# Results of attention on 64x32 places of the array, and the attention's two PSUM banks as separate tiles until the weights are decoded

## The chip, the core and the metric

The kernel runs on one core of one Trainium2 chip. A core has five engines with their own instruction queues: PE (TensorE, matmuls and transposes; its weight loads are listed as PEld), DVE (VectorE), ACT (ScalarE), POOL (GpSimd) and SP (SyncE), which here issues every DMA. They wait for each other through semaphores, and each works through its own instructions in the order in which they were written. Matmuls write to PSUM, eight banks of 128 partitions by 512 fp32 columns; DVE and ACT read and write PSUM too. The metric is the time of one execution on the device, in microseconds (us).

## The reference

Attention of 8 batches with 8 heads, 576 positions and head dimension 64, under a mask: in the first four heads a position sees itself and the 31 before it, in the last four every fourth of the 128 positions up to itself. The result, one row of 512 numbers per position, goes through a layer of two matmuls with a rational function between them:

```python
scores = scale * np.matmul(q, k.transpose(0, 1, 3, 2))
scores = np.where(masks[None], scores, -1e9)
attn = np.exp(scores - np.max(scores, axis=-1, keepdims=True))
attn = attn / (np.sum(attn, axis=-1, keepdims=True) + 1e-09)
x = np.matmul(attn, v)          # then (4608, 512)
h = x @ w_in                    # (4608, 2048)
P = a[0] + a[1] * h + a[2] * h**2 + a[3] * h**3
Q = 1.0 + np.abs(b[0]) * np.abs(h) + np.abs(b[1]) * h**2
out = (P / (Q + 1e-06)) @ w_out # (4608, 512)
```

w_in and w_out come as doubles, which the kernel turns into pairs of fp32 numbers itself (a decode of bit operations).

## The kernel before, in words

**Attention.** Each batch has six units (each 192 positions of 4 heads). A unit goes through a fixed chain: its q, k and v are loaded; PE multiplies q by k (scores); DVE adds the mask, takes the maximum and subtracts it (in some units of batches 0 and 1, PE adds the mask, and ACT takes the exponentials straight from PSUM); ACT takes exponentials, DVE sums and inverts (`recip`, lines 367 and 368); POOL normalizes (`norm`); PE transposes the weights (`transposes`, line 377); ACT or DVE copies them to SBUF (`place`, the tile p_T); PE multiplies v by them (`av`, the result); ACT and DVE split the result into a high part xh and a rest xl. Results of one unit and scores of the next are one step on PE. In batches 0 and 1 (`ROWS = 2`) a place holds two heads and the matmuls use all 128 rows and 64 columns of the array. From batch 2 on ("rows" units) two half arrays of 64 rows work side by side, each writing a bank of its own: the scores on places of 64 rows by 32 columns (eight at once), the results on places of 64 by 64 (four at once). These matmuls are fp32; the trace lists each as two weight loads and two matmuls.

**Two banks.** The scores and the transposes use the bank "att", the results the bank "dec". Batch 0 uses other banks too, for overlap. "dec" is also where DVE decodes the weights: a weight of 128x512 takes a scale on ACT, then `w_shift` (line 607), `w_low` and `w_sign` on DVE (in the trace the last two have the helper's line 216: `pair<-wi_raw,pair` and `wi_f<-wi_raw,pair`). att and dec are the two halves of one PSUM tile named `pair`; the framework sets semaphore waits by tile. The rows units need both halves as one tile, since DVE and ACT treat them with one instruction.

**The layer.** 144 tiles, each one of nine chunks of 512 positions by one of sixteen blocks of 128 hidden units: 12 matmuls for h, a chain on ACT, DVE and POOL for the rational function, 12 matmuls into four output banks (out0 to out3).

**The order.** All steps are put to a planner (`Plan`), which simulates the engines with costs that stand in the code and writes each engine's instructions in the order it finds. Its tables (`DUE`, `LATE`, `SLACK`) give ranks, `PLACE` tells which engine copies p_T, `EARLY_TILES` in how many tiles POOL may take a copy. SP's DMAs stand in one queue too. Helpers record most operations, so matmuls have line 207, ACT's line 210, DVE's lines 213 and 216, POOL's line 219, DMAs line 204.

Of the kernel before, what the change touches and what calls it, by code (L numbers as in the profile page):

```python
# [8 lines left out]
F32 = mybir.dt.float32  # L9
# [9 lines left out]
P = 128  # L19
# [6 lines left out]
BOTH, ON_ACT, ON_DVE = {"ACT": 450, "DVE": 500}, {"ACT": 450}, {"DVE": 500}  # L26


ON_PE = [[1, 0, 0, 1, 1, 1], [1, 0, 1, 1, 1, 0], [0, 0, 0, 0, 0, 0], [0, 0, 0, 0, 0, 0], [0, 0, 0, 0, 0, 0], [0, 0, 0, 0, 0, 0], [0, 0, 0, 0, 0, 0], [0, 0, 0, 0, 0, 0]]
PLACE = [(ON_ACT, ON_DVE), (ON_ACT, ON_ACT), (ON_ACT, ON_ACT), (ON_ACT, ON_DVE), (ON_ACT, ON_DVE), (ON_ACT, ON_DVE), (ON_ACT, ON_DVE), (ON_ACT, ON_DVE)]  # L30
DUE = [(1.15, 0.77), (7.09, 0.53), (31.18, 3.35), (45.13, 2.24), (56.94, 2.08), (78.73, 2.4), (94.03, 1.97), (106.25, 0.46)]

LATE = {"ab": -18.93, "ql": -5.42, "pl": 8.78, "qq": 10.97, "t1": 2.93, "t2": -2.65, "ln": -22.56, "ex": -6.33, "g0": 2.2, "g1": 0.06, "g2": -8.94, "gh": -36.44, "gl": 12.6, "out": 3.9}
SLACK = {"sc": -0.4, "qk0": 0.75, "v0": 0.39, "load": -2.47, "wi": 1.95, "wo": 0.71, "w": 0.5, "gl": 0.63, "out": 2.59}

EARLY_TILES = 40

ROWS = 2
LEFT = S - 512
# [38 lines left out]
class Plan:  # L78
# [3 lines left out]
    HOP = {"PE": 200.0, "ACT": 135.0, "DVE": 120.0, "POOL": 80.0, "SP": 0.0}  # L82
    TO_POOL, DUE_HOP, WINDOW = 70.0, 150.0, 100.0
    DMA_START, DMA_NS, DMA_RATE = 4000.0, 1600.0, 405.0
    PERIOD = 4082.0

    def __init__(self):
        self.ops, self.tags = [], {}
# [87 lines left out]
def tile_attention_moe(  # L176
# [17 lines left out]
    att = ctx.enter_context(tc.tile_pool(name="att", bufs=1))  # L194
    psum = ctx.enter_context(tc.tile_pool(name="psum", bufs=1, space=bass.MemoryType.PSUM))

    pin = tc.keep_in_program_order
    plan = Plan()  # L200
    op = plan.op
# [4 lines left out]
    def mm(o, lhs, rhs, start=True, stop=True):  # L206
        pin(nc.tensor.matmul(o, lhs, rhs, start=start, stop=stop))  # L207
# [44 lines left out]
    class Unit:  # L252
# [24 lines left out]

        def bank(self, tag, what):
            if tag in PAIR:
                return pair[:, PAIR[tag]]  # L280
            return psum.tile([P, 512], F32, tag=tag, name=f"{what}{self.n}", bufs=PS_BUFS[tag])

        def scores(self, tag, masked):
# [11 lines left out]
                mm(ps[64 * h : 64 * h + 64, cols], q_t[:, h, j, :], k_t[:, h, 32 * j : 32 * j + 64], start=not masked, stop=not masked or j == 5)  # L295

        def scores_rows(self):
            q_t = self.q.rearrange("p (g i c) -> p g i c", g=4, i=3)
            k_t = self.k.rearrange("p (g k) -> p g k", g=4)
            for i in range(3):  # L300
                for g in range(4):
                    for r in range(2):
                        half = slice(64 * r, 64 * r + 64)
                        mm(pair[32 * g : 32 * g + 32, r, 64 * i : 64 * i + 64], q_t[half, g, i], k_t[half, g, 32 * i : 32 * i + 64])

        def masks(self):
            for j, cnt, at in MASK_AT[self.u]:
# [11 lines left out]

        def blocks(self):  # L320
            if self.rows:
                return pair[:, :, :192].rearrange("p r (i k) -> p r i k", k=64)
            return self.s[:, :384].rearrange("p (j k) -> p j k", k=64)

        def small(self, tag):
# [62 lines left out]
        def av(self, tag):  # L388
            v_t = self.v.rearrange("p (i h e d) -> p i h e d", i=3, h=2, e=2)
            if self.rows:  # L390
                for i in range(3):
                    for h in range(2):
                        for e in range(2):
                            for r in range(2):
                                half = slice(64 * r, 64 * r + 64)
                                c0, c1 = 192 + 96 * h + 32 * i, 64 * h + 32 * e
                                mm(pair[64 * e : 64 * e + 64, r, c0 : c0 + 32], v_t[half, i, h, e, :], pT_rows[half, i, c1 : c1 + 32])
                return
            self.o = ps = self.bank(tag, "o_ps")
# [40 lines left out]
        def src(self, cols):  # L440
            first, cnt = cols
            if self.rows:
                o = pair[:, :, 192:384].rearrange("p r (h t) -> p h r t", h=2)
                if cnt > 96:
                    assert cnt == 192
                    return o
                r, t = divmod(first, 96)
                return o[:, :, r, t : t + cnt]
            return self.o[:, :384].rearrange("p (h t) -> p h t", h=2)[:, :, first : first + cnt]
# [14 lines left out]
        def plan(self, by, start):  # L464

            b, u = self.b, self.u
# [4 lines left out]
            rows = self.rows  # L471
            cold = 1.06 if start else 1.0
# [11 lines left out]
            ready = [lq, lk] + ([masked, identity] if on_pe else [])  # L484
            assert not (rows and on_pe)
            cost = 250 * on_pe
            scores = self.scores_rows if rows else lambda: self.scores(s_tag, on_pe)

            prev, Unit.open = Unit.open, None
            clear = []  # L490
            if prev and prev.rows != rows:
                clear = [close(prev), *decoded]
                prev = None
            if prev:
                sc = op({"PE": 1250 if rows else 1750 + cost}, 0, lambda e: (prev.av(prev.o_tag), scores()), *prev.placed, prev.lv, *ready)
                clear = prev.finish(sc)
            else:
                sc = op({"PE": 800 if rows else 1050 * cold + cost}, 0, lambda e: scores(), *ready, *clear)
            if on_pe:
                ma = mx = op({"DVE": 545}, 0, lambda e: self.max_bank(), sc)  # L500
                su = ex = sm = op({"ACT": 1750}, 0, lambda e: self.exp_bank(pp, pt), mx)
# [68 lines left out]

    def close(u):

        av = op({"PE": 800 if u.rows else 1050}, 0, lambda e: u.av(u.o_tag), *u.placed, u.lv)
        av.slack = 0.0
        eh, el = u.finish(av)
        if u.rows:
            plan.takes(av, "att", 1, [el])
        return el
# [24 lines left out]

    def w_shift(key):

        wb[key] = b = pair[:, PAIR["dec"]]
        pin(nc.vector.tensor_scalar(b.bitcast(I32), wf[key].bitcast(I32), 3, None, ALU.logical_shift_left))  # L607

    def w_low(key):
# [52 lines left out]
    class Tile:  # L662
# [8 lines left out]
        def h(self):  # L671
            xh, xl = x_tiles(self.c)
            w = wt["wi", self.ft]
            if self.bank in PAIR:
                ps = pair[:, PAIR[self.bank]]
            else:
                ps = psum.tile([P, 512], F32, tag=self.bank, name=f"h{self.i}", bufs=PS_BUFS[self.bank])
            self.ps = ps
            for kt in range(NK):
                wh, wl = w[:, 0, kt * P : (kt + 1) * P], w[:, 1, kt * P : (kt + 1) * P]  # L680
                mm(ps, wh, xh[:, kt, :], start=(kt == 0), stop=False)
                mm(ps, wh, xl[:, kt, :], start=False, stop=False)
                mm(ps, wl, xh[:, kt, :], start=False, stop=(kt == NK - 1))
# [113 lines left out]


    PAIR = {"att": 0, "dec": 1}
    pair = psum.tile([P, 2, 512], F32, name="pair")  # L800
    mask_t = const.tile([P, len(STRIP), 64], BF16, name="mask_t")
    ident = const.tile([P, P], F32, name="ident")
    ident_b = const.tile([P, P], BF16, name="ident_b")
# [166 lines left out]
```

## Time and profile before

| | |
|---|---|
| time, median of 3 runs | 968.23 us (966.24 to 968.71) |
| profiled execution, its own time | 968.85 us |
| its span (first to last instruction) | 967.0 us |
| PE busy | 917.1 us, 95% |
| PEld busy | 743.2 us, 77% |
| DVE busy | 707.3 us, 73% |
| ACT busy | 692.4 us, 72% |
| POOL busy | 464.8 us, 48% |
| mean granted PE clock | 0.975 |
| results of rows units, matmuls | 1728 records, 32.5 us |
| scores of rows units, matmuls | 1728 records, 26.1 us |

Busy time is a union: overlapping instructions of one engine count once. In rows of waits, "A <- B: total, times, longest" means that A's engine stood idle before A until B was done. In rows of the timeline the idle time before an instruction stands in brackets with what ended it. Times of POOL are rough, and the ends of matmuls are modelled; their starts are recorded.

### The profile page before, as it was taken

What the parts mean: (1) busy time and instruction counts of PE and PEld (TensorE: products, weight loads), DVE (VectorE), ACT (ScalarE), POOL (GpSimd) and SP (SyncE); (2) the same over time, 40 slices, a digit from 0 to 9 for tenths busy, and PEclk for the clock granted to TensorE, in tenths of its full rate; (3) what the DMA queues carried; (4) which work ended last, traced back from release to release, by engine and by line L of the source; (5) the groups of instructions that cost most, each with busy time, mean ns of one, the idle gap of its engine ahead of it and who ended that gap; (6) DMA issues with size and microseconds to landing.
All of it is one profiled execution on the core that took longest, in us unless ns stands there. A gap on an engine that the chain in (4) does not pass through costs nothing.

```text
span 967.0 us, 19505 instructions
## 1 busy us (share of the span) xinstructions
PE 917.1 (95%) x7645; PEld 743.2 (77%) x7645; DVE 707.3 (73%) x1273; ACT 692.4 (72%) x1205; POOL 464.8 (48%) x404
## 2 busy tenths in 40 slices
PE   6578789899999999999999999999999999999998
PEld 5465667678888877888888888888888888888876
DVE  5767789967877778778577776777677676657565
ACT  4666668866767677777777778767777777777765
POOL 3445456755555444444544445444454454444542
PEclk9977889999999999999999999999999999999999
DMA  9642560002332222311022121222112000001001
GB/s 335 252 150 68 192 269 22 1 20 72 116 116 82 70 73 72 110 48 66 1 81 71 38 73 44 73 72 72 43 74 72 18 22 23 1 1 45 0 1 44
DMA packets 26012, 72.53 MB, mean 75 GB/s; under 512 B 3008, under 2 KB 3904, under 8 KB 25920
## 3 DMA queue, kind: packets, MB, share of 16 engines
q1 hardware_dynamic: 25920, 71.28, 21.2%
q8 instruction: 60, 0.98, 0.4%
q14 instruction: 32, 0.26, 0.1%
HBM read 60.79 MB, written 10.49 MB: 74 GB/s over the span
## 4 chain that ended last, share of the span: by engine, by line
PE 75%; DVE 7%; ACT 3%; DMA 2%; POOL 1%; issue 1%; SPq 0%; POOLq 0%; ACTq 0%; DVEq 0%
PE out L207 34%; PE h L207 34%; PE pair L207 6%; DMA wo_raw<-in_w_out_dram 2%; DVE a L216 2%; PE pair L377 1%; ACT r L210 1%; DVE h L216 1%; DVE pair L216 1%; POOL a L219 1%; DVE pair L607 1%; DVE t L213 1%; DVE wo_f L216 1%; DVE xl L213 0%; ACT xh L210 0%
## 5 line engine op out<-in xcount | busy, mean ns | idle before, releaser
L207 PE MATMUL h<-xh,wi 128*128 128x512 f32 x1136 | 382.0, 398 | 12.7 <-DVE a L216 12.6
L207 PE MATMUL out<-gh,wo 128*128 128x512 f32 x1136 | 360.7, 399 | 1.0 <-POOL wo L219 0.8
L219 POOL TENSOR_TENSOR a<-r,a 128x512 f32<-128x512 f32 x141 | 182.1, 1291 | 321.8 <-ACT r L210 283.8
L207 PEld LDWEIGHTS h<-xh,wi 128*128 128x128 f32 x1136 | 216.0, 190 | 65.9 <-DVE a L216 18.9
L207 PEld LDWEIGHTS out<-gh,wo 128*128 128x128 f32 x1136 | 210.9, 190 | 44.9 <-POOL wo L219 1.1
L207 PE MATMUL h<-xl,wi 128*128 128x512 f32 x568 | 224.1, 395 | 0.0
L207 PE MATMUL out<-gl,wo 128*128 128x512 f32 x568 | 223.3, 393 | 0.0
L219 POOL TENSOR_TENSOR gl<-a,gh 128x512 fp32r<-128x512 f32 x141 | 184.3, 1307 | 25.3 <-ACT gh L210 22.7
L216 DVE SCALAR_TENSOR_TENSOR a<-a,r 128x512 f32<-128x512 f32 x141 | 98.9, 702 | 116.6 <-ACT r L210 115.4
L210 ACT ACTIVATE a<-h 128x512 f32<-128x512 f32 x140 | 83.5, 597 | 105.7 <-PE h L207 96.7
L216 DVE SCALAR_TENSOR_TENSOR h<-h,na_t,r 128x512 f32<-128x512 f32 x142 | 107.0, 754 | 50.2 <-ACT r L210 50.1
L210 ACT ACTIVATE r<-a,ln_bias 128x512 f32<-128x512 f32 x141 | 102.0, 723 | 56.3 <-POOL a L219 55.8
L207 PEld LDWEIGHTS out<-gl,wo 128*128 128x128 f32 x568 | 107.8, 190 | 23.2
L207 PEld LDWEIGHTS h<-xl,wi 128*128 128x128 f32 x568 | 108.1, 190 | 21.8 <-DVE xl L213 0.4
L210 ACT ACTIVATE r<-a,ab_t 128x512 f32<-128x512 f32 x141 | 114.6, 813 | 5.3 <-DVE a L216 3.2
L213 DVE TENSOR_TENSOR t<-t,h 128x512 f32<-128x512 f32 x142 | 96.8, 681 | 20.9 <-ACT t L210 19.5
L210 ACT ACTIVATE t<-h,na_t 128x512 f32<-128x512 f32 x142 | 109.6, 772 | 1.5 <-PE h L207 1.5
L216 DVE SCALAR_TENSOR_TENSOR h<-t,na_t,h 128x512 f32<-128x512 f32 x142 | 107.0, 754 | 3.9
L210 ACT ACTIVATE r<-r,exp_bias 128x512 f32<-128x512 f32 x144 | 103.9, 722 | 3.9
L210 ACT ACTIVATE gh<-a 128x512 fp32r<-128x512 f32 x126 | 79.5, 631 | 31.7 <-PE out L207 25.9
L216 DVE SCALAR_TENSOR_TENSOR a<-a,h 128x512 f32<-128x512 f32 x140 | 95.6, 683 | 2.8
L219 POOL TENSOR_TENSOR p<-p,sm 128x384 f32<-128x384 f32 x48 | 40.2, 837 | 60.8 <-DVE sm L368 34.3
(103 smaller groups left out, 720.3 us busy)
## 6 DMA issues: line engine op xcount, KB each, us to landing
v<-in_vp_dram SPq DMA_DIRECT2D x48, 384.0 KB, 3.4
qk<-in_qk_rows_dram SPq DMA_DIRECT2D x36, 448.0 KB, 4.7
out_dram<-os SPq DMA_DIRECT2D x36, 256.0 KB, 2.2
wi_raw<-in_w_in_dram SPq DMA_DIRECT2D x16, 512.0 KB, 8.6
wo_raw<-in_w_out_dram SPq DMA_DIRECT2D x16, 512.0 KB, 9.1
qk<-in_qk_dram SPq DMA_DIRECT2D x6, 608.0 KB, 4.7
q<-in_qk_dram SPq DMA_DIRECT2D x6, 384.0 KB, 6.9
k<-in_qk_dram SPq DMA_DIRECT2D x6, 224.0 KB, 7.0
```

Of the source, the lines that this page charges most:

```text
L207: pin(nc.tensor.matmul(o, lhs, rhs, start=start, stop=stop))
L210: pin(nc.scalar.activation(o, i, func, **kw))
L213: pin(nc.vector.tensor_tensor(o, x, y, op))
L216: pin(nc.vector.scalar_tensor_tensor(o, x, s, y, op0, op1))
L219: pin(nc.gpsimd.tensor_tensor(o, x, y, op))
L377: pin(nc.tensor.transpose(self.t[:, P * i : P * i + P], pf[:, P * i : P * i + P], ident))
L607: pin(nc.vector.tensor_scalar(b.bitcast(I32), wf[key].bitcast(I32), 3, None, ALU.logical_shift_left))
```

## The change

Four things change.

1. `av` of the rows units uses 64x32 places: the 64 rows of a result's half are two matmuls of 32 columns each, on two places, so 48 matmuls in the code in place of 24. They write the same numbers to the same places of PSUM, in an order that goes over the eight places.
2. att and dec are two tiles of a pool of their own as long as units of batches 0 and 1 and the decode use them (`two_banks` without `joined`). At the first scores of a rows unit that pool is closed and one tile of two banks is opened in its place (`join_banks`).
3. In batches 3 to 7 the copy of p_T goes from ACT to DVE (`PLACE`; the rows units use only the first entry).
4. The planner's tables and some of its costs have other numbers, and `EARLY_TILES` is 48.

```diff
-PLACE = [(ON_ACT, ON_DVE), (ON_ACT, ON_ACT), (ON_ACT, ON_ACT), (ON_ACT, ON_DVE), (ON_ACT, ON_DVE), (ON_ACT, ON_DVE), (ON_ACT, ON_DVE), (ON_ACT, ON_DVE)]
+PLACE = [(ON_ACT, ON_DVE), (ON_ACT, ON_ACT), (ON_ACT, ON_DVE), (ON_DVE, ON_ACT), (ON_DVE, ON_ACT), (ON_DVE, ON_ACT), (ON_DVE, ON_ACT), (ON_DVE, ON_ACT)]
...
-EARLY_TILES = 40
+EARLY_TILES = 48
...
-    PERIOD = 4082.0
+    PERIOD = 4051.0
...
+    early_banks = ExitStack()
+    apart = early_banks.enter_context(tc.tile_pool(name="psum_apart", bufs=1, space=bass.MemoryType.PSUM))
...
         def bank(self, tag, what):
             if tag in PAIR:
-                return pair[:, PAIR[tag]]
+                return two_banks(tag, f"{what}{self.n}", self.rows)
...
         def scores_rows(self):
+            join_banks()
...
-                        for e in range(2):
+
+                        for n in range(4):
                             for r in range(2):
-                                half = slice(64 * r, 64 * r + 64)
+                                half, e, d = slice(64 * r, 64 * r + 64), n // 2, slice(32 * (n % 2), 32 * (n % 2) + 32)
                                 c0, c1 = 192 + 96 * h + 32 * i, 64 * h + 32 * e
-                                mm(pair[64 * e : 64 * e + 64, r, c0 : c0 + 32], v_t[half, i, h, e, :], pT_rows[half, i, c1 : c1 + 32])
+                                mm(pair[0][32 * n : 32 * n + 32, r, c0 : c0 + 32], v_t[half, i, h, e, d], pT_rows[half, i, c1 : c1 + 32])
...
-        wb[key] = b = pair[:, PAIR["dec"]]
+        wb[key] = b = two_banks("dec", "%s_b%d" % key, False)
...
-    pair = psum.tile([P, 2, 512], F32, name="pair")
+    pair = []
+
+    def two_banks(tag, name, joined):
+        if not joined:
+            return apart.tile([P, 512], F32, tag=tag, name=name, bufs=1)
+        join_banks()
+        return pair[0][:, PAIR[tag]]
+
+    def join_banks():
+        if not pair:
+            early_banks.close()
+            late = ctx.enter_context(tc.tile_pool(name="psum_joined", bufs=1, space=bass.MemoryType.PSUM))
+            pair.append(late.tile([P, 2, 512], F32, name="pair"))
```

How the order and the waits move is shown at three places. In brackets stand the semaphores for which an instruction waits: DVE, PE, Activation, Pool, and DMAHW for loads.

**PE, the fourth unit of batch 1:** transposes (line 377, after the change 381), the first output group of a tile, results. Before:

```order
L377 MATMUL pair<-ident,p_911 128x128 [waits DVE_49,Pool_49]
L377 MATMUL pair<-ident,p_911 128x128 x2
L207 MATMUL out_0_0_676<-gh_894,wo_951 128x512 [waits Activation_49]
L207 MATMUL out_0_0_676<-gh_894,wo_951 128x512 [waits Pool_49]
L207 MATMUL out_0_0_676<-gl_927,wo_951 128x512
L207 MATMUL pair<-p_T,v_892 64x64 [waits DMAHW2_49,DVE_49]
```

With the change:

```order
L381 MATMUL t_ps_981<-ident,p_939 128x128 [waits Pool_49]
L381 MATMUL t_ps_981<-ident,p_939 128x128 x2
L210 MATMUL out_0_0_703<-gh_919,wo_978 128x512 [waits Activation_49]
L210 MATMUL out_0_0_703<-gh_919,wo_978 128x512 [waits Pool_49]
L210 MATMUL out_0_0_703<-gl_952,wo_978 128x512
L210 MATMUL o_ps_998<-p_T,v_917 64x64 [waits DMAHW2_49,DVE_49,Activation_49]
```

The order is the same. The transposes no longer wait for DVE, only for POOL's normalization; the results wait for ACT's copies by name, which before stood behind DVE's wait.

**DVE, the same time:** the last steps of one weight's decode and the three steps of the next (the weights' numbers differ between the kernels). Before:

```order
L216 SCALAR_TENSOR_TENSOR pair<-wo_raw_542,pair 128x512 [waits DMAHW1_49]
L216 SCALAR_TENSOR_TENSOR wo_f_802<-wo_raw_542,pair 128x512 [waits DVE_49]
L216 SCALAR_TENSOR_TENSOR h_819<-h_819,na_t,r_886 128x512 [waits Activation_49]
L607 TENSOR_SCALAR pair<-wi_f_834 128x512 [waits DVE_49]
L216 SCALAR_TENSOR_TENSOR pair<-wi_raw_544,pair 128x512 [waits DMAHW2_49,DVE_49,PE_49]
L216 SCALAR_TENSOR_TENSOR wi_f_834<-wi_raw_544,pair 128x512 [waits DVE_49,Activation_49]
```

With the change:

```order
L219 SCALAR_TENSOR_TENSOR wo_f_657<-wo_raw_549,wo_b_954 128x512
L612 TENSOR_SCALAR wi_b_976<-wi_f_837 128x512 [waits DVE_49]
L219 SCALAR_TENSOR_TENSOR h_848<-h_848,na_t,r_911 128x512 [waits Activation_49]
L219 SCALAR_TENSOR_TENSOR wi_b_976<-wi_raw_560,wi_b_976 128x512 [waits DMAHW2_49,DVE_49]
L219 SCALAR_TENSOR_TENSOR wi_f_837<-wi_raw_560,wi_b_976 128x512 [waits DVE_49]
```

The second step lost its wait for PE (the transposes), the third its wait for ACT (the copies of p_T). In the same way ACT's first copy of p_T waits for DVE before and for PE with the change.

**PE, the second rows unit:** results (p_T and v) and scores (qk) between output groups. Before:

```order
L207 MATMUL out_0_0_1405<-gl_2104,wo_1743 128x512 [waits Pool_49]
L207 MATMUL pair<-p_T,v_1268 64x32 [waits DMAHW1_49]
L207 MATMUL pair<-p_T,v_1268 64x32 x23
L207 MATMUL pair<-qk_1854 32x64 [waits DMAHW6_49]
L207 MATMUL pair<-qk_1854 32x64 x23
L207 MATMUL out_1_0_1414<-gh_2084,wo_1743 128x512 x2
```

With the change:

```order
L210 MATMUL out_0_0_1449<-gl_2164,wo_1795 128x512 [waits Pool_49]
L210 MATMUL pair<-p_T,v_1307 32x32 [waits DMAHW1_49]
L210 MATMUL pair<-p_T,v_1307 32x32 x47
L210 MATMUL pair<-qk_1914 32x64 [waits DMAHW6_49]
L210 MATMUL pair<-qk_1914 32x64 x23
L210 MATMUL out_1_0_1458<-gh_2144,wo_1795 128x512 x2
```

The result's 24 matmuls are 48, each with 32 columns of weights and 32 columns streamed; the place in the order is the same.

More of the change, by code (lines that the diff above doesn't have):

```diff
@@ L29 @@
 ON_PE = [[1, 0, 0, 1, 1, 1], [1, 0, 1, 1, 1, 0], [0, 0, 0, 0, 0, 0], [0, 0, 0, 0, 0, 0], [0, 0, 0, 0, 0, 0], [0, 0, 0, 0, 0, 0], [0, 0, 0, 0, 0, 0], [0, 0, 0, 0, 0, 0]]
-PLACE = [(ON_ACT, ON_DVE), (ON_ACT, ON_ACT), (ON_ACT, ON_ACT), (ON_ACT, ON_DVE), (ON_ACT, ON_DVE), (ON_ACT, ON_DVE), (ON_ACT, ON_DVE), (ON_ACT, ON_DVE)]
-DUE = [(1.15, 0.77), (7.09, 0.53), (31.18, 3.35), (45.13, 2.24), (56.94, 2.08), (78.73, 2.4), (94.03, 1.97), (106.25, 0.46)]
-LATE = {"ab": -18.93, "ql": -5.42, "pl": 8.78, "qq": 10.97, "t1": 2.93, "t2": -2.65, "ln": -22.56, "ex": -6.33, "g0": 2.2, "g1": 0.06, "g2": -8.94, "gh": -36.44, "gl": 12.6, "out": 3.9}
-SLACK = {"sc": -0.4, "qk0": 0.75, "v0": 0.39, "load": -2.47, "wi": 1.95, "wo": 0.71, "w": 0.5, "gl": 0.63, "out": 2.59}
-EARLY_TILES = 40
+PLACE = [(ON_ACT, ON_DVE), (ON_ACT, ON_ACT), (ON_ACT, ON_DVE), (ON_DVE, ON_ACT), (ON_DVE, ON_ACT), (ON_DVE, ON_ACT), (ON_DVE, ON_ACT), (ON_DVE, ON_ACT)]
+DUE = [(1.14, 0.78), (7.17, 0.52), (31.12, 3.35), (44.26, 2.11), (55.98, 1.84), (78.88, 1.84), (93.23, 1.71), (104.69, 0.27)]
+LATE = {"ab": -19.97, "ql": -10.42, "pl": 5.4, "qq": 18.68, "t1": 4.2, "t2": -2.51, "ln": -22.56, "ex": -3.7, "g0": 1.26, "g1": 0.06, "g2": -6.38, "gh": -35.31, "gl": 12.35, "out": 3.53}
+SLACK = {"sc": -0.4, "qk0": 0.66, "v0": 0.33, "load": -2.47, "wi": 2.03, "wo": 0.71, "w": 0.79, "gl": 0.63, "out": 2.59}
+EARLY_TILES = 48
 ROWS = 2
@@ L303, in scores_rows @@
                         half = slice(64 * r, 64 * r + 64)
-                        mm(pair[32 * g : 32 * g + 32, r, 64 * i : 64 * i + 64], q_t[half, g, i], k_t[half, g, 32 * i : 32 * i + 64])
+                        mm(pair[0][32 * g : 32 * g + 32, r, 64 * i : 64 * i + 64], q_t[half, g, i], k_t[half, g, 32 * i : 32 * i + 64])
         def masks(self):
@@ L321, in blocks @@
             if self.rows:
-                return pair[:, :, :192].rearrange("p r (i k) -> p r i k", k=64)
+                return pair[0][:, :, :192].rearrange("p r (i k) -> p r i k", k=64)
             return self.s[:, :384].rearrange("p (j k) -> p j k", k=64)
@@ L442, in src @@
             if self.rows:
-                o = pair[:, :, 192:384].rearrange("p r (h t) -> p h r t", h=2)
+                o = pair[0][:, :, 192:384].rearrange("p r (h t) -> p h r t", h=2)
                 if cnt > 96:
@@ L494, in plan @@
             if prev:
-                sc = op({"PE": 1250 if rows else 1750 + cost}, 0, lambda e: (prev.av(prev.o_tag), scores()), *prev.placed, prev.lv, *ready)
+                sc = op({"PE": 1370 if rows else 1750 + cost}, 0, lambda e: (prev.av(prev.o_tag), scores()), *prev.placed, prev.lv, *ready)
                 clear = prev.finish(sc)
             else:
-                sc = op({"PE": 800 if rows else 1050 * cold + cost}, 0, lambda e: scores(), *ready, *clear)
+                sc = op({"PE": 720 if rows else 1050 * cold + cost}, 0, lambda e: scores(), *ready, *clear)
             if on_pe:
@@ L571, in close @@
     def close(u):
-        av = op({"PE": 800 if u.rows else 1050}, 0, lambda e: u.av(u.o_tag), *u.placed, u.lv)
+        av = op({"PE": 1020 if u.rows else 1050}, 0, lambda e: u.av(u.o_tag), *u.placed, u.lv)
         av.slack = 0.0
@@ L674, in h @@
             if self.bank in PAIR:
-                ps = pair[:, PAIR[self.bank]]
+                ps = two_banks(self.bank, f"h{self.i}", True)
             else:
```

## The prediction

> **What bounds the kernel now.** I read the page's slices first, then the busy time by stage, then the waits of the first 222 us, then the timeline where those waits sit. The two rows of the page (40 slices of 24.2 us):
>
> ```profile
> PE   6578789899999999999999999999999999999998
> PEclk9977889999999999999999999999999999999999
> ```
>
> PE is full from the tenth slice on; before it, it idles, and its granted clock falls. By stage (busy us and instructions of each engine, then clock, DMA share, GB/s):
>
> ```profile
> 0.00:109.00 109.00, 76.37 (x717) 60.30 (x719) 72.64 (x152) 67.00 (x189) 49.34 (x58) 0.83 0.53 187
> 109.00:131.00 22.00, 18.76 (x109) 14.99 (x106) 18.10 (x36) 13.93 (x25) 12.80 (x12) 0.82 0.95 358
> 131.00:200.00 69.00, 59.71 (x291) 45.68 (x289) 63.61 (x103) 55.71 (x91) 44.83 (x36) 0.98 0.13 49
> 200.00:962.00 762.00, 761.15 (x6533) 621.62 (x6534) 552.91 (x985) 554.18 (x900) 357.82 (x299) 1.00 0.16 52
> ```
>
> Four stages. Up to 109 us nothing is full: PE 70%, DVE 67%, ACT 61%. A chain of single steps through the attention units sets the pace. From 109 to 131 us the last weights come in (DMA 95%). From 131 to 200 us DVE decodes them (63.6 of 69 us). From 200 us PE has no gap (761.2 of 762). So a microsecond won ahead of 109 us moves all that follows, and after 200 us only PE's own work counts.
>
> What the units wait for in the first 222 us (total us, times, longest us):
>
> ```profile
> PE pair L377 <- DVE pair L607: 7.0, 4, 2.8
> PE pair L377 <- DVE pair L216: 4.3, 1, 4.3
> DVE pair L216 <- PE pair L377: 4.6, 3, 2.8
> ACT p_T L210 <- DVE pair L216: 4.7, 4, 1.9
> DVE pair L607 <- ACT p L210: 4.0, 2, 2.0
> PE pair L207 <- DVE wi_f L216: 3.0, 2, 1.8
> PE pair L207 <- DVE wo_f L216: 1.2, 2, 0.8
> ```
>
> L377 transposes into the att bank; L607 and "DVE pair L216" write the dec bank. Neither needs the other's data: they wait because both banks are one tile. The last two rows, the results in dec waiting for a weight's last decoding step, are true ones and stay.
>
> **The early stage.** The fourth unit of batch 1 shows how such waits chain (start, us, engine, line):
>
> ```profile
> 87.55 0.83 POOL L219 TENSOR_TENSOR p<-p,sm 128x384 f32<-128x384 f32 x1 [2.08 <-DVE sm L368]
> 89.30 0.69 DVE L607 TENSOR_SCALAR pair<-wi_f 128x512 int32<-128x512 int32 x1
> 90.13 0.88 PE L377 MATMUL pair<-ident,p 128*128 128x128 f32 x3 [2.81 <-DVE pair L607]
> 91.04 0.69 DVE L216 SCALAR_TENSOR_TENSOR pair<-wi_raw,pair 128x512 int32<-128x512 int32 x1 [1.06 <-PE pair L377]
> 91.77 0.98 ACT L210 ACTIVATE p_T<-pair 64x384 f32<-64x384 f32 x2 [1.90 <-DVE pair L216]
> 92.78 0.69 DVE L216 SCALAR_TENSOR_TENSOR wi_f<-wi_raw,pair 128x512 int32<-128x512 int32 x1 [1.05 <-ACT p_T L210]
> 93.53 1.55 PE L207 MATMUL pair<-p_T,v 128*64 128x64 f32 x24 [1.24 <-DVE wi_f L216]
> ```
>
> The normalized weights are there at 88.38, the transposes start at 90.13. Then decode step, copies, decode step go one behind the other, though the copies and the decode have nothing in common. With two tiles the transposes start at about 88.45, the three decode steps run back to back from 89.30 (3 x 0.69, to 91.4), the copies run beside them, and the results start at 91.4 in place of 93.53: 2.1 us. The same in the first, third and fifth unit:
>
> ```profile
> 42.92 0.83 POOL L219 TENSOR_TENSOR p<-p,sm 128x384 f32<-128x384 f32 x1 [1.75 <-ACT r L210]
> 45.38 0.87 PE L377 MATMUL pair<-ident,p 128*128 128x128 f32 x3 [4.32 <-DVE pair L216]
> 48.05 1.55 PE L207 MATMUL pair<-p_T,v 128*64 128x64 f32 x24 [1.79 <-DVE wi_f L216]
> ...
> 68.34 0.70 DVE L607 TENSOR_SCALAR pair<-wi_f 128x512 int32<-128x512 int32 x1 [1.95 <-ACT p L210]
> 70.39 0.19 DVE L368 RECIPROCAL sm<-sm 128x6 f32<-128x6 f32 x1
> 72.02 0.52 PE L377 MATMUL pair<-ident,p 128*128 128x128 f32 x3 [2.36 <-DVE pair L607]
> ...
> 102.96 0.83 POOL L219 TENSOR_TENSOR p<-p,sm 128x384 f32<-128x384 f32 x1 [5.01 <-DVE sm L368]
> 104.25 0.52 PE L377 MATMUL pair<-ident,p 128*128 128x128 f32 x3 [0.99 <-DVE pair L607]
> 107.29 1.55 PE L207 MATMUL pair<-p_T,v 128*64 128x64 f32 x24 [0.77 <-DVE wo_f L216]
> ```
>
> First unit: inputs at 43.75, transposes at 45.38, so 1.6 us. Third: the shift sat 1.95 us behind exponentials that read the other bank, and the reciprocal, the normalization and the transposes queue behind it; they come about 2 us earlier, and PE's own gap there, 2.36, goes almost whole: I take 2.3. Fifth: the decode's three steps and one more DVE step of 0.75 from 103.41 end at 106.2, so 1.1 in place of 107.29. The 7.0 us of L607 leave 7.0 - 2.4 - 2.8 - 1.0 = 0.8 for a unit of batch 0. The second unit's results wait for PE's own tiles, and I count nothing. Sum 0.8 + 1.6 + 2.3 + 2.1 + 1.1 = **7.9 us**. Next late is then the decode itself, the two true rows. Bounds: if each earlier transpose meets another queue, only the 3.0 + 1.2 us in front of the results are won (4.2); if all goes, 7.0 + 4.3 + 4.2 = 15.5.
>
> It is passed on: the last 16 weights stand on the SP queue behind the sixth unit's v, which waits for the fifth unit's results.
>
> ```profile
> 108.88 0.33 SPq L204 DMA_DIRECT2D v<-in_vp_dram  x1
> 109.26 1.61 SPq L204 DMA_DIRECT2D wi_raw<-in_w_in_dram  x2
> 111.87 9.08 DMA wo_raw<-in_w_out_dram
> ```
>
> They start 1.6 us after 107.29 and move with it; so do their landing and the decode from 131 us. New waits: a bank's next tile waits until the last one has been read, the same readers as before. On PE the first scores of a batch-1 unit now wait for its own transposes, long done: nothing.
>
> **The results on smaller places.** 35 units have results and scores together; here is one, PE's matmuls and, as PEld, its weight loads. The three middle rows are the same scores with the view cut at 247.90, 248.055 and 248.145 us:
>
> ```profile
> 246.87 0.90 PE L207 MATMUL pair<-p_T,v 64*64 64x32 f32 x48
> 247.70 0.30 PEld L207 LDWEIGHTS pair<-qk 64*32 64x32 f32 x33
> 247.70 0.45 PEld L207 LDWEIGHTS pair<-qk 64*32 64x32 f32 x36
> 247.70 0.55 PEld L207 LDWEIGHTS pair<-qk 64*32 64x32 f32 x47
> 247.70 0.73 PE L207 MATMUL pair<-qk 64*32 64x64 f32 x48
> 248.36 0.74 PE L207 MATMUL out<-gh,wo 128*128 128x512 f32 x2
> ```
>
> Results and scores hold PE from 246.87 to 248.36, 1.49 us. Each fp32 matmul of the code is two records, so 24 are 48; the change makes 48 of the result's 24, 96 records. It also drops the switch between 64x64 and 64x32 places inside the pair (the 1.49 us contain it). The results now cost 0.83 / 48 = 17 ns a record, the scores on 64x32 places 0.66 / 48 = 14. But that is not one rate: 33 loads start in the first 0.20 us (6 ns each), then 3 in 0.155 us, then 11 in 0.09 us (8.2 ns). I read this as a full queue that drains and then a steady supply. For 96 + 48 = 144 loads in one mode: 0.20 + 0.155 + 108 x 0.0082 = 1.24 us, and from the last load (about 248.155) to the next tile 0.205: **1.45 us**, 0.04 less than 1.49. Times 35: -1.4 us. The last unit's results alone, 96 loads: 0.20 + 0.155 + 60 x 0.0082 = 0.85 against about 0.69 of its 0.90: +0.2. Together -1.2. Bounds: all at 6.1 ns, 0.88 + 0.205 = 1.08, -14 us in all. The pause of 0.155 us after every 33: 4 x 0.355 + 0.205 = 1.63, +5. If the mean behind the first 33 (15 loads in 0.255 us, 17 ns) held for the other 111: 0.20 + 111 x 0.017 + 0.205 = 2.29, +28. I take 8.2 ns after one pause, the rate seen last, with the queue empty.
>
> [...]
>
> **The rest.** Batches 3 to 7 move the copy of the transposed weights from ACT to DVE:
>
> ```profile
> L210 ACT ACTIVATE p_T<-pair 128x384 f32<-128x384 f32 x36 | 17.5, 486 | 2.1 <-PE pair L377 2.0
> L222 DVE COPY p_T<-t_ps 64x384 f32<-64x384 f32 x3 | 1.7, 561 | 0.7 <-ACT p_T L210 0.6
> ```
>
> 30 x 0.56 = 17 us on an engine busy 553 of 762, hidden behind the tiles between transposes and results. The shortest cover, two output groups, is about 1.4 us and takes the copy with one DVE step ahead of it (0.56 + 0.75). If that failed by 0.1 to 0.3 us in the ten units with so short a cover it would cost 1 to 3 us; I take 0. The new tables leave PE's order in the first eleven units as it was but for an output group or two; later order is free while PE is full. 0, within 2 either way.
>
> Sum against the profiled execution: 968.85 - 7.9 - 1.2 = **959.7 us**. That execution stands 0.6 above the median of the runs, 968.23, so 959.4 sits between both bases.
>
> **The rivals.**
> - *Faster still.* The supply keeps the 6 ns, or the halved clock of the early stage mostly goes with the gaps. For: PE's clock is 0.83 up to 109 us and 1.00 in the full stage. Against: the 8.2 ns are there in a unit of the trace. 968.85 - 7.9 - 14 = 947, or with 15.5 early 952. [...]
> - *The early gain is lost.* The last weights or the decode are what counts, and they don't start earlier. For: DMA 95%, DVE 92% in those stages. Against: the SP rows, where the first of these weights goes out behind 107.29. 968.85 - 1.2 = 967.6.
> - *Slower: PE is starved of instructions.* Twice as many small matmuls, and a queue that runs dry after 33 loads. For: the drop to 3 loads in 0.155 us. Against: the 8.2 ns behind it. Each ns more per load costs 108 x 35 = 3.8 us, so it decides from 9.1 / 3.8 = 2.4 ns more, 10.6 ns a load; at 17 ns for all behind the first 33, 968.85 - 7.9 + 28 = 989. [...]
>
> **How the numbers follow.** Chances: forecast (953 to 964.5) 0.62, faster still 0.17, gain lost 0.11, starved PE 0.10. The range 950 to 967 holds the forecast, half of the faster case and most of the lost gain. A measurement of this kernel can tell about 0.3%, 2.9 us, so faster means below 965.3. Faster: forecast 0.62, faster still 0.17 and a little of the other two, 0.82. Within 0.3%: most of the lost gain, 0.09. Slower: 0.09.
>
> **What would show it.** Early: L377 no longer waits for L612 (the shift), no wait of the p_T copies for DVE, the fifth unit's results at about 100 us, the first of the last weights at about 101, the last scores ahead of the full stage some 8 us earlier. Places: 96 and 48 records in about 1.45 us to the next tile and no gap between them; 1.6 or more is the slower case. PE still without gaps after 200 us. I am wrong if the early stage ends less than 4 us earlier, if the pair takes over 1.7 us, or if PE waits for DVE's p_T copies.

## The result, and the profile after

The changed kernel takes 952.12 us (median of 4 runs, 949.98 to 954.06) against 968.47 us of the kernel before beside it: ratio 0.9835, 95% interval 0.9807 to 0.9862. That is faster by 16.4 us, or 1.7%. The profiled execution has 949.98 us and a span of 948.2, so 18.9 us less than the profiled execution before; it is the fastest of the four, so what follows is read from a gain somewhat larger than that of the medians.

The slices of the page (23.7 us each now) show PE filling up from the eighth slice, two earlier than before, and a granted clock that stays at 0.9 or more in every slice:

```profile
PE   6699788999999999999999999999999999999998
PEclk9999999999999999999999999999999999999999
```

By stage, with the cuts moved to where the same work lies now: the issue of the last weights, their landing, and the first scores of a rows unit (these came at 192 us before, a little ahead of the 200 us at which the prediction cuts):

```profile
0.00:88.00 88.00, 67.92 (x727) 54.70 (x729) 71.57 (x151) 65.44 (x188) 49.87 (x59) 0.94 0.65 232
88.00:109.00 21.00, 18.52 (x113) 14.88 (x109) 20.47 (x41) 16.07 (x28) 14.80 (x14) 1.00 0.99 383
109.00:167.00 58.00, 49.24 (x201) 37.84 (x200) 53.47 (x84) 47.51 (x78) 38.32 (x31) 0.97 0.12 47
167.00:944.00 777.00, 769.18 (x8343) 627.64 (x8341) 574.46 (x1028) 547.39 (x879) 366.35 (x307) 1.00 0.16 52
```

About the work that took 109 us takes 88, and the clock in it is 0.94 instead of 0.83. But the last row isn't full: PE is busy for 769.2 of 777 us, so it idles for 7.8. Before, from the same scores on (192 to 962 us), it was busy for 768.2 of 770, and idle for 1.8. Both kernels issue 3456 matmuls of 128x512 in the layer, so the start of the same one in both says how far the change is ahead:

```text
128x512 matmul no.     25     121     193     265     401    1001    3456
before (us)         53.72  100.38  130.53  152.58  190.19  350.43  962.75
changed (us)        48.83   81.27  105.49  127.90  165.50  331.74  943.98
ahead (us)            4.9    19.1    25.0    24.7    24.7    18.7    18.8
```

(At no. 1001 the changed kernel has one pair of results and scores more behind it, some 1.8 us of work; at the other columns both have done the same.) The change gains 24.7 us before the full stage and gives 6 of them back in it. Two questions follow: why the early gain is three times the 7.9 us of the prediction, and what the full stage loses.

**The early stage.** This is the same unit of batch 1 as in the prediction, now at 67 us (timeline of the changed kernel; in the names s_ps and t_ps stand for the bank att, o_ps and wi_b or wo_b for dec):

```profile
67.20 0.92 PE L210 MATMUL o_ps<-p_T,v 128*64 128x64 f32 x24
...
70.08 0.55 DVE L337 TENSOR_REDUCE mx<-s_ps 128x6 f32<-128x384 f32 x1
...
71.39 0.42 DVE L216 TENSOR_TENSOR xl<-o_ps,xh 128x256 fp32r<-128x256 f32 x1
...
72.04 0.69 DVE L612 TENSOR_SCALAR wo_b<-wo_f 128x512 int32<-128x512 int32 x1
...
73.56 0.19 DVE L372 RECIPROCAL sm<-sm 128x6 f32<-128x6 f32 x1
...
74.78 0.55 PE L381 MATMUL t_ps<-ident,p 128*128 128x128 f32 x3
...
77.12 0.92 PE L210 MATMUL o_ps<-p_T,v 128*64 128x64 f32 x24
```

From the results of one unit to those of the next it takes 9.92 us. Before, the rows of the same steps, some of them not among those shown in the prediction:

```profile
79.61 0.92 PE L207 MATMUL pair<-p_T,v 128*64 128x64 f32 x24
...
83.07 0.56 DVE L333 TENSOR_REDUCE mx<-pair 128x6 f32<-128x384 f32 x1 [0.85 <-ACT xh L210]
...
85.77 0.42 DVE L213 TENSOR_TENSOR xl<-pair,xh 128x256 fp32r<-128x256 f32 x1 [1.28 <-ACT p L210]
...
87.22 0.19 DVE L368 RECIPROCAL sm<-sm 128x6 f32<-128x6 f32 x1
```

With 93.53 for the next results that is 13.92. Of the 4.0 us of difference, 2.75 lie between the reciprocal and the next results (6.31 us before, 3.56 now): there the prediction had looked, and had counted 2.1. The other 1.25 lie ahead of the reciprocal, in DVE's own queue: the maximum in att waited until ACT had read the result in dec, and the split of the result in dec waited until ACT had taken the exponentials from att. DVE's waits of this kind in the first 200 us, beside the 4.6 and 4.0 us shown in the prediction:

```profile
DVE xl L213 <- ACT p L210: 3.6, 2, 2.3
...
DVE pair L213 <- ACT xh L210: 2.5, 2, 1.3
DVE wi_f L216 <- ACT p_T L210: 2.5, 2, 1.4
...
DVE wo_f L216 <- ACT p_T L210: 1.5, 2, 1.0
...
DVE mx L333 <- ACT xh L210: 0.8, 1, 0.8
```

All seven rows together are 19.5 us. With the change none of them is left; what DVE waits for most is now the layer's own chain, "DVE h L219 <- ACT r L213: 10.9, 8, 2.4" (3.0 before). So the 19.5 us are not a gain of that size: a part of them has become another wait.

It is passed on as the prediction said. The last weights stand on SP's queue behind the sixth unit's v, which waits for the fifth unit's results, now at 86.74 instead of 107.29:

```profile
87.69 0.33 SPq L207 DMA_DIRECT2D v<-in_vp_dram  x1
88.07 1.98 SPq L207 DMA_DIRECT2D wi_raw<-in_w_in_dram  x2
```

**The full stage.** An undisturbed pair of results and scores starts at 556.07 and the next tile at 557.51, 1.44 us, as forecast:

```profile
556.07 0.99 PE L210 MATMUL pair<-p_T,v 64*32 64x32 f32 x94
...
556.90 0.69 PE L210 MATMUL pair<-qk 64*32 64x64 f32 x46
557.51 0.73 PE L210 MATMUL out<-gh,wo 128*128 128x512 f32 x2
```

The pair overlaps now: the first scores start at 556.86, the last results at 556.90. Measured from the last large matmul ahead of the pair to the first behind it, 32 of the 35 pairs take 1.77 us, where all 35 took 1.81: -0.038 us each, -1.3 in all. The other three pairs take 2.1, 3.2 and 3.9 us. What PE waits for from 192 us on:

```profile
PE pair L210 <- issue: 3.1, 2, 1.9
PE h L210 <- DVE a L219: 1.0, 3, 0.4
PE h L210 <- DVE pair L216: 0.9, 1, 0.9
PE h L210 <- issue: 0.8, 1, 0.8
PE pair L381 <- POOL p L222: 0.5, 1, 0.5
...
```

"issue" is a wait for which the profile finds no releaser. It falls into the middle of the scores, whose only wait stands on their first matmul, or on a large matmul just behind a pair. The longest:

```profile
587.51 0.66 PE L210 MATMUL pair<-qk 64*32 64x64 f32 x42
...
590.04 0.30 PE L210 MATMUL pair<-qk 64*32 64x64 f32 x4 [1.87 <-issue]
```

I counted PE's records (loads, matmuls, semaphore instructions) up to each of these stalls. The first record behind them is no. 2754, 4290, 6594, 12738 and 13506 of the trace: each is 256 n + 194, with n = 10, 16, 25, 49 and 52. The row put down to "DVE pair L216" is the second of them. The page lists the transfers that fetch instructions, 60 of them before and 73 now:

```profile
q8 instruction: 73, 1.20, 0.5%
```

That is 16.4 KB each, and 18,813 PE records / 73 = 258 instructions each. 15,368 / 60 before are 256. So the stalls lie whole multiples of 256 instructions apart, the size of one transfer by these counts; I call the stretch between two such places a block. In the trace PE goes on 2.3 to 2.7 us after the last transfer ahead of the stall has begun. A pair is now 288 instructions in 1.45 us; before it was 192 in 1.49. Four of the stalls, as idle time, are 1.27, 0.91, 0.76 and 1.87 us, and the pair of the fifth takes 0.34 us more than an undisturbed one: 5.2 in all. The gaps behind DVE and POOL are 1.3 us more than before. The account: -24.7 - 1.2 (places) + 5.2 + 1.3 = -19.4, against -18.9 measured; 0.5 us stays unexplained. The runs below divide the loss in another way, between the tables and the places.

### The profile page after: what moved, and what is told of

The parts are those of the page before. It is cut to its first block, busy times and chain, and to the rows that moved or that the text cites. A ratio compares the mean times of both kernels' runs of the same rounds, so it can differ in the third digit from the quotient of the medians.

```text
span 948.2 us, 22991 instructions
## 1 busy us (share of the span) xinstructions
PE 905.2 (95%) x9373; PEld 735.1 (78%) x9373; DVE 720.0 (76%) x1301; ACT 677.3 (71%) x1172; POOL 469.3 (49%) x409
## 4 chain that ended last, share of the span: by engine, by line
PE 80%; DVE 10%; ACT 5%; issue 2%; DMA 1%; POOL 1%; SPq 0%; ACTq 0%; POOLq 0%; DVEq 0%
PE h L210 36%; PE out L210 36%; PE pair L210 6%; DVE a L219 2%; ACT r L213 1%; DVE h L219 1%; PE pair L381 1%; DVE xl L216 1%; PE s_ps L210 1%; ACT p L213 1%; DVE mx L337 1%; DVE t L216 1%; ACT t L213 1%; DVE wo_b L219 1%; ACT a L213 1%
## 5 line engine op out<-in xcount | busy, mean ns | idle before, releaser
L219 DVE SCALAR_TENSOR_TENSOR a<-a,r 128x512 f32<-128x512 f32 x141 | 98.2, 697 | 114.6 <-ACT r L213 112.4
L213 ACT ACTIVATE r<-a,ln_bias 128x512 f32<-128x512 f32 x141 | 102.2, 725 | 72.5 <-POOL a L222 72.3
L213 ACT ACTIVATE a<-h 128x512 f32<-128x512 f32 x140 | 83.6, 597 | 87.1 <-PE h L210 86.4
L219 DVE SCALAR_TENSOR_TENSOR h<-h,na_t,r 128x512 f32<-128x512 f32 x142 | 107.0, 754 | 43.1 <-ACT r L213 43.0
L213 ACT ACTIVATE r<-a,ab_t 128x512 f32<-128x512 f32 x141 | 114.7, 813 | 5.5 <-DVE a L219 3.5
L219 DVE SCALAR_TENSOR_TENSOR h<-t,na_t,h 128x512 f32<-128x512 f32 x142 | 107.2, 755 | 4.1
L213 ACT ACTIVATE t<-h,na_t 128x512 f32<-128x512 f32 x142 | 110.0, 774 | 0.1
L213 ACT ACTIVATE r<-r,exp_bias 128x512 f32<-128x512 f32 x144 | 103.8, 721 | 3.6
L216 DVE TENSOR_TENSOR t<-t,h 128x512 f32<-128x512 f32 x142 | 96.9, 682 | 11.2 <-ACT t L213 10.1
L213 ACT ACTIVATE gh<-a 128x512 fp32r<-128x512 f32 x123 | 77.7, 632 | 38.6 <-PE out L210 28.5
L219 DVE SCALAR_TENSOR_TENSOR a<-a,h 128x512 f32<-128x512 f32 x140 | 95.4, 682 | 2.5
```

Of the source, the lines that this page charges most:

```text
L213: pin(nc.scalar.activation(o, i, func, **kw))
L216: pin(nc.vector.tensor_tensor(o, x, y, op))
L219: pin(nc.vector.scalar_tensor_tensor(o, x, s, y, op0, op1))
```

## Experiments

The theory to be tested has three parts: the separate banks alone make the early gain; the smaller places gain 1.3 us in their own time and lose more at ends of instruction blocks; the tables do nothing. The rivals: the early gain needs the new tables, or is the clock's; the stalls belong to the new order, or to the small places as such.

**One part of the change at a time.** The banks alone (in the kernel before):

```diff
-                return pair[:, PAIR[tag]]
+                return two_banks(tag, f"{what}{self.n}", self.rows)
...
-        wb[key] = b = pair[:, PAIR["dec"]]
+        wb[key] = b = two_banks("dec", "%s_b%d" % key, False)
```

> The kernel before with the two separate banks alone; tables and places as before. By the prediction's sum (7.9 us of false waits) 960 us. By what the changed kernel's trace shows (its early stage ends 24.7 us earlier at the same count of matmuls), if the banks alone do it: about 944 us, with half-clock time ahead of 140 us falling from 44 us to some 10 to 15. If the new tables are needed for it: 955 or more. No stall of PE inside or just behind results and scores.

Measured: 946.53 us (944.47 to 947.62), ratio 0.9768 (0.9752 to 0.9784). The banks alone are faster than the whole change. The 265th large matmul starts 20.4 us earlier than before, no pair stalls, and the last weights are issued at 90.82 instead of 109.26:

```profile
90.82 1.85 SPq L207 DMA_DIRECT2D wi_raw<-in_w_in_dram  x2
```

It stays 2.5 us above the 944 that were expected if the banks alone make the early gain, and the half-clock time ahead of 140 us falls from 44.4 to 20.5 us, not to 10 to 15: the tables have a part in the early gain.

The places alone (in the kernel before):

```diff
-                        for e in range(2):
+                        for n in range(4):
...
-                                mm(pair[64 * e : 64 * e + 64, r, c0 : c0 + 32], v_t[half, i, h, e, :], pT_rows[half, i, c1 : c1 + 32])
+                                mm(pair[32 * n : 32 * n + 32, r, c0 : c0 + 32], v_t[half, i, h, e, d], pT_rows[half, i, c1 : c1 + 32])
```

> The kernel before with the results on 64x32 places alone. By the prediction's term: -1.2 us, about 967. By a theory that PE's instructions come in blocks of 256 and that 288 instructions in 1.45 us can use up what is there: each pair of results and scores 1.77 us from the last large matmul ahead of it to the first behind, against 1.81, but 2 to 5 of the 35 pairs stall by 0.3 to 2.1 us, each where a block ends about 20 to 50 instructions into the pair: -1.2 plus 2 to 6, so 968 to 973.

Measured: 972.89 us (971.38 to 974.31), ratio 1.0047 (1.0030 to 1.0064): slower by 4.4 us. 32 pairs take 1.77 us, and PE waits for

```profile
PE pair L207 <- issue: 2.5, 2, 1.5
PE h L207 <- issue: 1.1, 2, 0.9
PE h L207 <- DVE a L216: 0.9, 2, 0.5
...
```

Seven stalls lie at block ends, each in or just behind a pair into which a block ended 22, 23, 37, 39, 48, 50 or 51 instructions in; PE stalls at the end of the next block, 256 instructions later, when the pair is nearly through. No other pair stalls by more than 0.1 us. Two to five stalls were expected; three of the seven are only 0.1 to 0.2 us. Behind the stall at 660 us the granted clock is halved for 3.4 us, and large matmuls start 427 ns apart instead of some 230 (226 to 227 for most of them at full clock in the trace of the kernel before, 427 at half), which costs some 1.6 us more by an estimate from the seven or eight of them.

The tables, costs and `PLACE` alone:

```diff
-PLACE = [(ON_ACT, ON_DVE), (ON_ACT, ON_ACT), (ON_ACT, ON_ACT), (ON_ACT, ON_DVE), ...
+PLACE = [(ON_ACT, ON_DVE), (ON_ACT, ON_ACT), (ON_ACT, ON_DVE), (ON_DVE, ON_ACT), ...
...
-    PERIOD = 4082.0
+    PERIOD = 4051.0
```

> The kernel before with the new tables, costs and places of the p_T copy alone; one tile for both banks, results on 64x64 places. By the prediction 0 within 2 us: 966 to 970. If the new tables carry part of the early gain: 955 to 964. If the tables were made for the separate banks and hurt without them: 970 or more.

Measured: 968.62 us, ratio 1.0003 (0.9993 to 1.0012). They gain 3.3 us early and lose 3 in the full stage.

The changed kernel with the places of before:

```diff
-                                mm(pair[0][32 * n : 32 * n + 32, r, c0 : c0 + 32], v_t[half, i, h, e, d], pT_rows[half, i, c1 : c1 + 32])
+                                mm(pair[0][64 * e : 64 * e + 64, r, c0 : c0 + 32], v_t[half, i, h, e, :], pT_rows[half, i, c1 : c1 + 32])
```

> The changed kernel with the results back on 64x64 places; the order of all other instructions is the same. If the stalls of PE in the full stage (five of them, 5 to 6 us in all) come from the number of instructions in a burst (288 against 192 now), they go, and the pairs cost 1.3 us more: 952.1 - 5.5 + 1.3 = 948 us, with no wait of PE inside or just behind a pair. If they come from the new order or the tables, they stay: 952.1 + 1.3 = 953.4.

Measured: 947.16 us (945.38 to 948.36), ratio 0.9780 (0.9765 to 0.9795). All 35 pairs take 1.80 to 1.82 us, and the waits for "issue" are gone in the same order of instructions:

```profile
PE pair L381 <- POOL p L222: 1.3, 2, 0.7
PE h L210 <- DVE a L219: 0.9, 3, 0.4
PE pair L210 <- DVE pair L219: 0.5, 1, 0.5
```

So the parts add up to nearly the whole: banks -22, tables 0, places +4 to +5, against -16.4. The new order is not what stalls. But it does lose time: from the first scores of a rows unit to the last large matmul the traces have 770.7 us before, 769.9 with the banks alone, 773.6 with the tables alone and 773.6 here, and 776.6 in the changed kernel. About half of the 6 us that the full stage gives back belongs to the tables, which win about as much ahead of it, and half to the places.

**Is it the count of instructions?** The changed kernel with 226 PE instructions more, ahead of everything, while PE waits for its first load. The only thing it changes in the full stage is where a block ends:

```diff
+    def shift():
+        ps = psum.tile([P, 512], F32, tag="h", name="shift", bufs=PS_BUFS["h"])
+        for i in range(113):
+            mm(ps[:32, :32], ident_b[:, :32], ident_b[:, :32])
...
     identity = op({"POOL": 1000}, -89, lambda e: make_idents())
+    op({"PE": 10}, -86, lambda e: shift(), identity)
```

> The changed kernel with 113 small matmuls (226 PE instructions, 32x32, their result is overwritten) ahead of the first scores, while PE waits for the mask's load; all else in the same order. It changes nothing in the full stage but where the blocks of 256 instructions end: 30 instructions further on in each pair. By the theory of the blocks, a pair stalls only if a block ends 22 to 51 instructions into it. In the changed kernel those were the pairs at 201, 250, 326, 587 and 613 us (31, 45, 39, 25 and 23 instructions in); shifted they have 61, 75, 69, 55 and 53 and run through or lose at most 0.4 us, and only the pair at 640 us, 9 before and 39 now, stalls, by about 1 us. So 952.1 - 5.5 + 1.2 = 947.8 us, between 946.5 and 949.5. If the five stalls belong to the places, to the new order or to loads, they stay where they were: 952.

Measured: 947.85 us (947.56 to 951.18), ratio 0.9793 (0.9773 to 0.9814). All five stalls are gone, and PE waits for nothing by "issue" from 190 us on:

```profile
PE pair L381 <- POOL p L222: 1.3, 2, 0.8
PE h L210 <- DVE a L219: 1.1, 3, 0.4
PE pair L210 <- DVE pair L219: 0.5, 1, 0.5
```

More work made the kernel 4.3 us faster by the medians; the two were timed beside the kernel before and not beside each other, and their intervals overlap a little. The traces say it more firmly: the full stage takes 772.7 us instead of 776.6, while the early stage ends 1.6 us later. One part of the expectation failed: the pair at 637 us, with an end 39 instructions in, runs through.

The same as a forecast for another program: separate banks and small places with the tables of before, and a number of dummy matmuls chosen from counts in other traces, once for few stalls (41) and once for many (77). Beside the edits shown above it has:

```diff
+        for i in range(41):
```

> The kernel before with the separate banks and the results on 64x32 places, tables as before, and 41 small matmuls (82 PE instructions) ahead of the first scores. From the counts of instructions in the traces of the kernels with one change each, a block of 256 ends 22 to 51 instructions into a pair in two of the 35 pairs only: the 12th (44 instructions in) and the 33rd (29). The theory of the blocks has PE stall there, by 0.2 to 1.5 us each, and nowhere else but for up to 0.3 us in the 10th (52): 946.5 (the banks alone) - 1.3 (places) + 1.5 = 946.7 us, between 945 and 948.5. If the places cost 4.4 us whatever the count (as they did without the banks, 972.9 against 968.5): 951.

Measured: 949.06 us (947.80 to 950.34), ratio 0.9800 (0.9786 to 0.9815). Both pairs that were named stall, by 0.6 and 1.7 us; so does one that was not (the 5th, by 1.1 us, 251 instructions in; the block before had ended 5 instructions ahead of that pair), which accounts for a part of the 2.4 us by which it is above the sum; it is 0.6 outside the bounds.

With 77 in place of 41:

```diff
-        for i in range(41):
+        for i in range(77):
```

> The same kernel with 77 small matmuls (154 PE instructions) ahead of the first scores. Now a block ends 22 to 51 instructions into seven pairs: the 2nd (24), 4th (34), 6th (50), 15th (48), 17th (34), 20th (49) and 26th (23). The theory of the blocks has PE stall in or just behind these, by 1 to 2 us where it is 23 to 35 and by 0.1 to 0.5 where it is 48 to 50, and nowhere else: 946.5 - 1.3 + 6 = 951 us, between 949 and 953, 4 us more than with 41 matmuls for 36 matmuls that PE does while it waits. If the count doesn't matter, both kernels take the same time.

Measured: 952.55 us (951.96 to 953.90), ratio 0.9838 (0.9822 to 0.9855), 3.5 us more for 36 matmuls more. Not all of that is block ends: in the profiled executions, 5.0 us apart, the first scores of a rows unit already start 2.35 us later (171.26 against 168.91), for a reason that no run shows, and the full stage takes 775.5 us instead of 772.9. Five of the seven named pairs stall, the two with 49 and 50 run through, and no other stalls. The waits of PE from 190 us on:

```profile
PE pair L210 <- issue: 4.0, 2, 2.5
PE out L210 <- issue: 1.0, 1, 1.0
...
PE h L210 <- issue: 0.2, 1, 0.2
```

Over the five kernels with 288 instructions a pair, 22 of 175 pairs had a block end 22 to 51 instructions in, and 19 of them stalled; of the other 153 one did by more than 0.1 us. In three kernels with 192 a pair (before, banks alone, old places) none of 105 did. That the block counts is shown; the rule of 22 to 51 is a fit to these programs. Where it was used as a forecast (the three kernels with idle matmuls), seven of the ten pairs that it named stalled, and one that it didn't name.

**Is it the clock?** The kernel before with idle work for PE, matmuls that add zeros to an output bank (six at each of nine places, 54 in all), where PE waits anyway (before, 10.5 us ahead of the transposes from 34.5 to 109 us):

```diff
+    def fill():
+        if open_out:
+            o = min(open_out)
+            for _ in range(6):
+                mm(open_out[o], ident_b, zero_b.to_broadcast([P, 16, 32]), start=False, stop=False)
...
-            tr = op({"PE": 350 * cold}, 0, lambda e: self.transposes(t_tag), no, identity)
+            tr = op({"PE": 350 * cold}, 0, lambda e: (fill() if b == 1 else None, self.transposes(t_tag)), no, identity)
```

> [...] If the half clock of the early stage (44 us ahead of 140 us) costs time of its own, the half-clock time falls below some 25 us and the kernel is faster although PE does more: 960 to 966 us. If the half clock only shows the waits and costs nothing of its own, the time stays or grows: 968.5 to 975.

Measured: 967.29 us (965.15 to 970.38), ratio 0.9992 (0.9979 to 1.0005). The granted clock of the early stage rises from 0.83 to 0.92:

```profile
0.00:109.00 109.00, 82.50 (x786) 61.72 (x787) 73.44 (x153) 68.55 (x192) 51.08 (x61) 0.92 0.53 189
```

and PE does 6 us more in it, yet the time doesn't move by more than it can be measured. The half-clock time ahead of 140 us falls from 44 to 24 us; if that was worth something, the added work took it back. Not much of it can have: from 34.5 to 109 us the transposes still wait for DVE's decode for 7.4 us, where they waited for 10.5 before, so a large part of the added work lies in time that was idle. The banks, with a similar fall of the half-clock time, gained 22 us, so this speaks against the clock as the main part; how small its part is, the run doesn't show.

**Two attempts at a still faster kernel.** The old places and old `PLACE` in the changed kernel, which puts the copies of p_T back on ACT:

```diff
-PLACE = [(ON_ACT, ON_DVE), (ON_ACT, ON_ACT), (ON_ACT, ON_DVE), (ON_DVE, ON_ACT), ...
+PLACE = [(ON_ACT, ON_DVE), (ON_ACT, ON_ACT), (ON_ACT, ON_ACT), (ON_ACT, ON_DVE), ...
```

> The changed kernel with results on 64x64 places and the p_T copies of all batches on the engines of before (ACT in batches 3 to 7). If the waits left in the full stage (2.9 us of gaps against 0.9 before) come from the copies on DVE, they go: 947.2 - 2 = 945 us. If they come from the other tables, they stay: 947, or more, since the planner's other numbers go with the copies on DVE.

Measured: 948.96 us (948.41 to 949.28), ratio 0.9796 (0.9782 to 0.9811). The gaps of the full stage stay (3.1 us against 2.9), so the copies on DVE are not what causes them.

The banks alone with those new tables that act early:

```diff
-DUE = [(1.15, 0.77), (7.09, 0.53), ...
-SLACK = {"sc": -0.4, "qk0": 0.75, "v0": 0.39, ...
+DUE = [(1.14, 0.78), (7.17, 0.52), ...
+SLACK = {"sc": -0.4, "qk0": 0.66, "v0": 0.33, ...
```

> The kernel before with the separate banks, and of the new tables only what acts in the early stage (SLACK and the due times of batches 0 and 1); results on 64x64 places. The early stage of the changed kernel ends 3.8 us earlier than with the banks alone (24.2 against 20.4 us ahead of the kernel before), and its full stage gives 2 to 3 us of it back through waits. If those two come from different tables, this kernel has the gain without the loss: 946.5 - 3.8 = 943 us. If they belong together: 946 to 948.

Measured: 960.45 us (958.80 to 960.74), ratio 0.9910 (0.9892 to 0.9929). A miss by 17 us. The planner now puts the fifth unit of batch 1 later: its results come at 97.61, the last weights are issued at 98.95, and PE then waits 11.7 us for the tiles' chain between 100 and 200 us:

```profile
PE h L210 <- DVE a L219: 11.7, 5, 6.0
```

It fits the view that the issue of the last weights sets the early stage's end: it is 8 us later than with the banks alone (90.82). But the 401st large matmul starts 14 us later (183.32 against 169.77), so the issue is not all of it; what the other 6 us are stays open.

The fastest kernel measured is the one with the banks alone, 946.5 us; the old places in the changed kernel (947.2) can't be told from it.

## Why the prediction was right, and where its sizes were off

**Direction and route: right.** The false waits between the two banks go, the last weights' issue moves with the fifth unit's results, and all behind moves along: the run with the banks alone shows it. 952.1 lies in the range of 950 to 967, but 7 us below the forecast and just outside its own band, 953 to 964.5; it is the 952 that the rival "faster still" names for an early gain of 15.5 us. That it meets this number is luck, since neither the early gain nor the full stage is as it was priced there. The signs that were named came: no transposes wait for the shift, no copy of p_T waits for DVE's decode, the pair takes 1.44 us. The fifth unit's results were to come at 100 us and came at 87.

**The early term, 7.9 us: mis-sized; it is 20.4 with the banks alone and 24.7 in the change.** The step that failed is the sum over units, 0.8 + 1.6 + 0 + 2.3 + 2.1 + 1.1. It counted what was seen between the normalized weights and the results, with one wait of DVE ahead of them (1.95 us, in the third unit), and left the rest of the unit as it was. From one unit's results to the next the run with the banks alone gains 4.5 us up to the first unit, where the sum has 0.8 + 1.6, and then 1.0, 4.4, 3.6 and 4.2 where it has 0, 2.3, 2.1 and 1.1. The bounds failed in the same place: the upper one, 7.0 + 4.3 + 4.2 = 15.5, adds up PE's gaps. The waits of DVE and ACT for the other bank delay the reciprocal, the next decode and the tiles' steps behind them in the queue, also where PE has other work at that moment. In the unit of the worked example 1.25 of 4.0 us were such waits, and in the second unit, for which I counted nothing, the results went from 14.6 to 12.8 us behind those of the first. DVE's seven rows alone add up to 19.5 us; the table in the prediction showed two of them, and the sum used them only where they stood in its own timelines.

**"It is passed on": right, and more than one to one.** The fifth unit's results came 20.6 us earlier, the last weights 21.2, the first scores of a rows unit 24.7 (192.09 to 167.40). The tables have a part in the last 4 us: with the banks alone the three numbers are 17.8, 18.4 and 20.4, and there 2.0 of the last 2.6 are already won by the sixth unit's results (121.62 before, 101.80).

**The places, -1.2 us: right as far as it went.** 1.44 us to the next tile against 1.45 forecast, -1.3 us for 35 pairs, +0.12 against +0.2 for the last unit. The working was a serial one, though: in the trace the last results and the first scores alternate, 94 result records in 0.80 us (8.5 ns each) and the scores at about 11 ns, as before, and not at the 8.2 ns of the sum; the end of the pair came sooner behind them and made up for it.

**"PE without gaps after 200 us": wrong.** That is the rival of the starved PE, with another mechanism. I looked for it in the rate of loads, where it would have cost every pair something, and found a steady 8.2 ns that speaks against it. What the five pairs that lose 5.2 us have in common is a block's end 23 to 45 instructions in; that PE waits there for its next instructions is my reading of the transfers' times, and no run shows it directly. The prediction had the cause (twice as many small matmuls) and not the unit in which it is paid. With it, the places cost 4.4 us on their own instead of gaining 1.2.

**The tables, 0 within 2: right** (1.0003), but as two effects of 3 us that cancel, neither of which was seen. **The copies on DVE, 0: right**; putting them back won nothing.

**"Faster still", through the clock: the symptom came, the price did not.** The clock is up in the slices as that rival said, and the time fell almost as low as it said, but through the waits. With a clock of 0.92 and the waits in place the kernel stays at 967.3.

So the forecast came out near for a reason that no part of it showed: an early gain three times as large, less a loss of 6 us in the full stage, of which one half, the places', had been thought of and dismissed, and the other, the tables', had not.

## What to carry to other kernels

Where one tile holds two things that have nothing to do with each other, look at the false waits of every engine that touches it, not only at those of the engine that sets the end: a wait in a queue delays all behind it (here 1.25 of the 4.0 us of one unit). Count a burst in instructions as well as in time: where PE runs through many of them without long matmuls between (here 288 stalled now and then, and 192 did not), look for waits put down to "issue" in mid-group, and compare the count with the instructions in one of the profile's instruction transfers (here 256). Splitting a matmul into smaller ones that take the same time is then not free (here it cost 4.4 us on its own).

## What the hardware showed that was not expected

The profile lists transfers of instructions, 16.4 KB each: 73 for the 18,813 PE records of the changed kernel, 60 for 15,368 before, so 258 and 256 records a transfer. In the changed kernel PE resumes 2.3 to 2.7 us after the last transfer ahead of a stall has begun, and it issued the 288 small instructions of an undisturbed pair in 1.45 us. If that transfer is the one for the next block, as the times suggest but no run shows, the fetch of one block took longer there than the use of another. What starts a transfer, and why one pair with an end at 39 ran through and another stalled whose block had ended 5 instructions ahead of it, stays open; other transfers were not varied.

113 idle matmuls ahead of the first scores made the full stage of one kernel 3.8 us shorter, and 36 more made that of another 2.6 us longer. So small edits of PE's program, which move the places of the block ends, changed the full stage by 0.3 to 0.5% of its time.
